# The sixth block of a per-head product, 40 rows and columns, or 120 that overlap the fifth

## The chip, the cores and the metric

The kernel runs on one core of one Trainium2 chip. The metric is the device time of one execution in microseconds, the median of several runs. Before the change it is 207.66 us (three runs, 207.59 to 207.98).

## What is computed

```python
xn = layernorm(x)                                   # x: 1 x 2048 x 640
q, k, v = split(xn @ wqkv)                          # 32 heads of 20 columns each
phi = lambda t: where(t > 0, t + 1, exp(t)) + 1e-6
pq, pk = phi(q), phi(k)
kv  = einsum("bhsd,bhse->bhde", pk, v)              # one 20 x 20 matrix per head
z   = einsum("bhsd->bhd", pk)
num = einsum("bhqd,bhde->bhqe", pq, kv)
den = einsum("bhqd,bhd->bhq", pq, z)[..., None] + 1e-6
attn  = (num / den) @ wo                            # heads joined to 640 columns
dense = gelu(xn @ w1 + b1) @ w2 + b2                # 640 -> 1536 -> 640
out = x + attn + dense                              # bfloat16 in and out
```

## The kernel before

The 2048 tokens are 16 tiles of 128, the 640 columns 5 tiles of 128. A small planner records every instruction of each engine in the order of the program text, works out which semaphores it has to wait for, and emits each engine's list as it stands. So the order on each engine is the order in which the Python code calls it. PSUM is eight banks of 512 fp32 columns, given out in turn by `take`; a matmul that gets a bank waits until its last reader is done.

TensorE goes through these stages one after the other:

- from 0 to 60 us: layernorm, transposes, and the first dense layer with gelu (`h_unit`, L357).
- 60 to 82: the keys, `phi(xn @ wk)` for 16 token tiles (L494), stored in PK.
- 82 to 104: GT, the product of the normalized tokens and PK over all tokens (L530), 640 x 640. The values are never formed: kv of a head is `wv.T @ GT` for that head's columns.
- 104 to 130: the queries in four chunks of 512 tokens (`q_chunk`, L542, 25 matmuls with 512 moving columns each). After a chunk's matmuls into one bank, `phi` runs on ScalarE (exp, L481) and VectorE (L482, L484) and leaves PQ.
- Between chunks 0 and 1, `kvt_step` makes the kv matrices. Inside chunk 2, after each of its five column tiles, `mt_block(nb)` multiplies them by 128 columns of wo.
- 130 to 205: the output. For each token tile, twelve pairs of matmuls with W2 and five with Msb (L643, the last tile in L679); in between, `den_step` (L590) gives the denominators, whose inverse is spread by a DMA (`rden_dma`) and multiplied into PQ (`rden_scale`). `x_again` reads x once more for the residual sum, after the last query matmul.

The 32 heads are cut into blocks of six heads, that is GW = 120 columns; 640 columns are NG = 6 blocks, five of 120 columns and a last one of gw[5] = 40 (two heads). `kvt_step` computes for block i, over five contraction tiles k, `Wqkv[v columns of i].T @ GT[columns of i]` into a 120 x 120 piece of a bank (40 x 40 for the last block). Blocks 0 to 3 go into one bank, blocks 4 and 5 into the next (`parts`). VectorE then multiplies with `maskKV`, a band of 20 x 20 ones along the diagonal, since only a head's own columns count, and writes KVT (L565): once for blocks 0 to 3, once for block 4, once for block 5.

`mt_block(nb)` has one matmul per block, with `Wo[rows of i, 128 columns]` as the stationary operand and KVT[i] as the moving one (L574): the contraction is over the block's 120 rows, 40 in the last. ScalarE copies the first bank to MT (L581), VectorE the second (L584), and a transposing DMA puts it into Msb (L586). The Wo rows come in two DMAs on SP's queue: blocks 0 to 4, then block 5; after them only W2 is queued among the weights.

In a matmul's shape, `128*40` in the profile is the stationary operand, 128 contraction rows and 40 columns, and `128x40` the moving operand, 40 columns long.

Of the kernel before, what the change touches and what calls it, by code (L numbers as in the profile page):

```python
# [5 lines left out]
ALU = AluOpType  # L6
ACT = mybir.ActivationFunctionType
P = 128
# [104 lines left out]
def bass_parallel_sum__linear_attn_block__dense_activation_gelu__prompt_kernel(  # L113
    nc: bass.Bass, A_x, A_wqkv, A_wo, B_x, B_w1, B_b1, B_w2, B_b2, out):
    Batch, S, D = A_x.shape
# [17 lines left out]
    GW = 6 * DH  # L133
    NG = -(-D // GW)
    gw = [min(GW, D - GW * i) for i in range(NG)]

    with contextlib.ExitStack() as es:
        sb = lambda *a, **k: es.enter_context(nc.sbuf_tensor(*a, **k))
# [13 lines left out]
        KVT = W1f[:, DT * D:DT * D + NG * GW].rearrange("p (g d) -> p g d", g=NG)  # L152
        MT = W1f[:, DT * D + NG * GW:DT * D + NG * GW + DT * D].rearrange("p (b d) -> p b d", b=DT)
        Wqkv = sb("Wqkv", [P, DT, 3 * D], BF16)
        W2 = sb("W2", [P, JT, D], BF16)
        Wo = sb("Wo", [P, NG, D], BF16)
# [9 lines left out]
        maskKV = sb("maskKV", [P, GW], BF16)  # L166
# [17 lines left out]
        def take(n):  # L184
            b = ring[0]
            if n == 2 and b % 2:
                b += 1
            b %= 8
            ring[0] = (b + n) % 8
            return b  # L190

        def bank(b, lo=0, hi=512):
            return ps[:, b * 512 + lo: b * 512 + hi]
# [16 lines left out]
        r_Wo = [R_("Wo%d" % i) for i in range(2)]  # L210
# [25 lines left out]
        def dma_w(eng, dst, src, res):  # L236
            Pl.ins(eng, lambda e: e.dma_start(dst, src), writes=[res], dma=True)
# [23 lines left out]
        dma_w("sync", Wqkv[:, :, 2 * D:3 * D], wqv[:, :, 2 * D:3 * D], r_Wv)  # L261
        dma_w("sync", b2bc[:], B_b2.rearrange("(a d) -> a d", a=1).partition_broadcast(P).rearrange("p a d -> p (a d)"), r_b2)
        dma_w("sync", Wo[0:GW, 0:NG - 1, :], A_wo[0:GW * (NG - 1), :].rearrange("(g p) n -> p g n", p=GW), r_Wo[0])
        dma_w("sync", Wo[0:gw[-1], NG - 1, :], A_wo[GW * (NG - 1):D, :], r_Wo[1])
        dma_w("sync", W2[:], B_w2.rearrange("(k p) n -> p k n", p=P), r_W2)

        g = "gpsimd"
# [221 lines left out]
        for t in range(NT):  # L489
            b = take(2)  # L490
# [36 lines left out]
        for f in range(DT):  # L527
            b = take(2)
# [24 lines left out]
        def kvt_step():  # L553
            for gs in parts:
                b = take(1)
                Pl.ins("tensor", [(lambda e, k=k, i=i, b=b, g0=gs[0]: e.matmul(  # L556
                    bank(b, GW * (i - g0), GW * (i - g0) + gw[i])[0:gw[i], :],
                    Wqkv[:, k, 2 * D + GW * i:2 * D + GW * i + gw[i]],
                    GTb[:, k, GW * i:GW * i + gw[i]], start=(k == 0), stop=(k == DT - 1)))
                    for i in gs for k in range(DT)], reads=[r_Wv] + r_GT, writes=[B_[b]])  # L560
                for lo, hi, w in ([(0, G1, GW)] if gs[0] == 0 else [(G1, NG - 1, GW), (NG - 1, NG, gw[-1])]):
                    n = hi - lo
                    src = bank(b, GW * (lo - gs[0]), GW * (lo - gs[0]) + n * w)[0:w, :].rearrange("p (g d) -> p g d", g=n)
                    msk = maskKV[0:w, 0:w].unsqueeze(1).to_broadcast([w, n, w])
                    Pl.ins(v, lambda e, lo=lo, hi=hi, w=w, src=src, msk=msk: e.tensor_tensor(  # L565
                        out=KVT[0:w, lo:hi, 0:w], in0=src, in1=msk, op=ALU.mult),
                        reads=[B_[b], r_masks], writes=[r_KVT] + r_W1)

        def mt_block(nb):
            for h, gs in enumerate(parts):  # L570
                b = take(1)
                n = gw[gs[0]] * (len(gs) - 1) + gw[gs[-1]]
                m0, m1 = GW * gs[0] // DT, (GW * gs[0] + n) // DT
                Pl.ins("tensor", [(lambda e, i=i, b=b, g0=gs[0]: e.matmul(  # L574
                    bank(b, GW * (i - g0), GW * (i - g0) + gw[i]), Wo[0:gw[i], i, nb * P:(nb + 1) * P],
                    KVT[0:gw[i], i, 0:gw[i]], start=True, stop=True)) for i in gs],
                    reads=r_Wo + [r_KVT], writes=[B_[b]])
                dst = MT[:, nb, :].rearrange("p (j m) -> p j m", j=DT)[:, :, m0:m1]
                src = bank(b, 0, n).rearrange("p (m j) -> p j m", j=DT)
                if h == 0:  # L580
                    Pl.ins("scalar", lambda e, dst=dst, src=src: e.activation(dst, src, ACT.Copy),  # L581
                           reads=[B_[b]], writes=[r_MT[nb][h]])
                else:
                    Pl.ins(v, lambda e, dst=dst, src=src: e.tensor_copy(dst, src),  # L584
                           reads=[B_[b]], writes=[r_MT[nb][h]])
            Pl.ins("sync", lambda e: e.dma_start_transpose(Msb[:, :, nb * P:(nb + 1) * P], MT[:, nb, :]),  # L586
                   reads=r_MT[nb], writes=[r_M[nb]] + ([r_zsum, r_zhl] if nb == 0 else []), dma=True)
# [37 lines left out]

        q_chunk(0)
        kvt_step()
        q_chunk(1)
        q_chunk(2, mt_block)
        q_chunk(3)  # L630
        for c in range(NC):
# [17 lines left out]
        def out_w2(t, lo=0, hi=JT, b=None):  # L649
            b = take(2) if b is None else b  # L650
            for i in range(lo, hi):
                Pl.ins("tensor", [mm(b, t, i, 0), mm(b, t, i, 1)], reads=mm_reads(t, i), writes=B_[b:b + 2],
                       mark=(i == JT - 1))
            return b
# [47 lines left out]
        for t in range(4, NT - 1):  # L702
            b = out_w2(t)
# [47 lines left out]
```

## Time and profile before

| | us |
|---|---|
| median of three runs | 207.66 |
| profiled execution | 208.03 |
| its span, first to last instruction | 206.8 |
| TensorE, weight loads busy | 139.4 |
| VectorE busy | 113.2 |
| ScalarE busy | 72.5 |
| L542, query matmuls, busy | 22.4 |
| L556, `kvt_step` matmuls, from 109.0 to | 110.8 |
| L574, first of `mt_block`, starts at | 117.2 |
| L574, last of `mt_block`, starts at | 123.9 |

The profile is of one execution, which took 208.03 us, 1.2 more than its span and 0.37 more than the median. Its lines give a start, a length and a count; a line of the timeline with a count over one runs from the first one's start to the last one's end. PE is the matmuls, PEld the weight loads that run beside them. Matmuls are pipelined and their recorded ends are modelled, so two records can overlap: where one instruction keeps the next one back, it is seen in the starts. The granted TensorE clock was 1.0.

### The profile page before, as it was taken

Reading aid. Unit: us, or ns where it says so; the run is one execution under the profiler, and the core shown is the slowest. Engines: PE = TensorE matmul, PEld = TensorE weight load, DVE = VectorE, ACT = ScalarE, POOL = GpSimd, SP = SyncE. Lnnn points to the kernel's source line nnn. Section 1 sums busy time; section 2 is a strip of 40 time slices with the busy share of each in tenths; the row PEclk is TensorE's granted clock in tenths of the full one; section 3 lists DMA queues with packets and bytes.
Section 4 is the critical chain, followed back from the end, with each engine's and each line's share of the span. In section 5 each row is a group of like instructions: output and inputs, shape, how many; then the busy total and the mean of one; then the engine's idle time right before and its main releaser. Section 6 shows DMA issues by size and latency. Waiting matters only on the chain.

```text
span 206.8 us, 3760 instructions
## 1 busy us (share of the span) xinstructions
PE 203.0 (98%) x1510; PEld 139.4 (67%) x1517; DVE 113.2 (55%) x231; ACT 72.5 (35%) x136; POOL 15.0 (7%) x46
## 2 busy tenths in 40 slices
PE   7999999999999999999999999999999999999996
PEld 2799987444457777777756565577777777777775
DVE  4668777200007888999288878474593522522332
ACT  3588887666676555111153566100000000000000
POOL 3143344300000000000000000000000000000000
PEclk9999999999999999999999999999999999999999
DMA  6993844599930000000300034682212111010002
GB/s 182 354 348 70 71 95 87 85 348 275 305 111 0 0 3 0 0 0 3 63 0 2 3 72 87 202 305 54 67 63 59 61 41 55 32 35 32 32 35 65
DMA packets 26579, 19.13 MB, mean 93 GB/s; under 512 B 13761, under 2 KB 26561, under 8 KB 26561
## 3 DMA queue, kind: packets, MB, share of 16 engines
q1 hardware_dynamic: 26265, 18.62, 32.7%
q10 hardware_dynamic: 296, 0.27, 0.5%
q8 instruction: 12, 0.20, 0.4%
q14 instruction: 6, 0.05, 0.1%
HBM read 12.62 MB, written 2.62 MB: 74 GB/s over the span
## 4 chain that ended last, share of the span: by engine, by line
PE 96%; DVE 1%; DMA 1%; issue 0%; DVEq 0%
PE ps L643 34%; PE ps L357 24%; PE ps L542 11%; PE ps L530 11%; PE ps L494 11%; PE ps L679 2%; PE ps L389 1%; DMA xPK<-in_A_x_dram 1%; PE ps L574 1%; DVE stats L313 1%; PE ps L556 1%; PE ps L590 1%; PE ps L378 0%; PE ps L341 0%; PE ps L300 0%
## 5 line engine op out<-in xcount | busy, mean ns | idle before, releaser
L643 PE MATMUL ps<-W,HG 128*128 128x320 bf16 x360 | 51.0, 299 | 0.0
L357 PE MATMUL ps<-xnT,W 128*128 128x256 bf16 (+2 forms) x382 | 50.4, 293 | 0.2
L643 PEld LDWEIGHTS ps<-W,HG 128*128 128x128 bf16 x360 | 35.1, 98 | 14.2 <-issue 0.4
L357 PEld LDWEIGHTS ps<-xnT,W 128*128 128x128 bf16 x385 | 33.8, 98 | 15.9
L361 ACT ACTIVATE HG<-ps,b1c 128x256 bf16<-128x256 f32 (+2 forms) x77 | 38.0, 515 | 12.7 <-PE ps L357 10.3
L662 DVE TENSOR_TENSOR out_sb<-ps,xnT 128x640 bf16<-128x640 f32 x15 | 12.4, 824 | 34.9 <-PE ps L643 34.6
L481 ACT ACTIVATE ek<-ps 128x512 bf16<-128x512 f32 (+1 forms) x36 | 23.2, 644 | 20.7 <-PE ps L542 11.5
L482 DVE TENSOR_SCALAR ek<-ek 128x512 bf16<-128x512 bf16 (+1 forms) x36 | 11.0, 307 | 27.4 <-ACT ek L481 26.1
L542 PE MATMUL ps<-xnT,Wqkv 128*128 128x512 bf16 x96 | 22.4, 381 | 0.3 <-issue 0.2
L643 PE MATMUL ps<-Msb,PQ 128*128 128x320 bf16 x150 | 22.3, 299 | 0.0
L494 PE MATMUL ps<-Wqkv,xnT 128*128 128x320 bf16 x160 | 21.9, 299 | 0.0
L530 PE MATMUL ps<-xPK,xn_tm 128*128 128x320 bf16 x160 | 21.9, 299 | 0.0
L494 PEld LDWEIGHTS ps<-Wqkv,xnT 128*128 128x128 bf16 x160 | 15.6, 98 | 6.3
L530 PEld LDWEIGHTS ps<-xPK,xn_tm 128*128 128x128 bf16 x160 | 15.6, 98 | 6.1
L643 PEld LDWEIGHTS ps<-Msb,PQ 128*128 128x128 bf16 x150 | 14.6, 98 | 5.7
L542 PEld LDWEIGHTS ps<-xnT,Wqkv 128*128 128x128 bf16 x100 | 11.3, 118 | 8.7
L313 DVE BATCH_NORM_STATS2 stats<-xPK 128x6 f32<-128x320 bf16 x32 | 14.7, 470 | 2.7 <-DMA xPK<-in_A_x_dram 2.7
L484 DVE SCALAR_TENSOR_TENSOR PQ<-ps,ek 128x512 bf16<-128x512 f32 x20 | 13.8, 692 | 2.1
L484 DVE SCALAR_TENSOR_TENSOR xPK<-ps,ek 128x640 bf16<-128x640 f32 x16 | 13.2, 824 | 1.7
L517 DVE TENSOR_TENSOR Msb<-Msb,xPK 128x640 f32<-128x640 f32 x14 | 11.6, 826 | 0.5
L323 POOL TENSOR_TENSOR rstd<-aggr,mhalf 128x1 f32<-128x1 f32 x16 | 9.1, 567 | 15.8 <-DVE aggr L321 15.8
L534 ACT ACTIVATE W<-ps 128x640 bf16<-128x640 f32 x5 | 3.5, 703 | 18.2 <-PE ps L530 18.2
(61 smaller groups left out, 92.7 us busy)
## 6 DMA issues: line engine op xcount, KB each, us to landing
xnT<-in_A_x_dram SPq DMA_DIRECT2D x4, 640.0 KB, 6.8
Wqkv<-in_A_wqkv_dram SPq DMA_DIRECT2D x3, 800.0 KB, 6.6
out_dram<-out_sb SPq DMA_DIRECT2D x15, 160.0 KB, 1.8
W<-in_B_w_dram SPq DMA_DIRECT2D x1, 1920.0 KB, 14.9
W<-in_B_w_dram SPq DMA_DIRECT2D x2, 640.0 KB, 7.4
xPK<-in_A_x_dram SPq DMA_DIRECT2D x2, 640.0 KB, 9.1
Wo<-in_A_wo_dram SPq DMA_DIRECT2D x1, 750.0 KB, 11.8
xPK<-in_A_x_dram SPq DMA_DIRECT2D x4, 160.0 KB, 4.6
```

The costliest lines, as they stand in the source:

```text
L313: Pl.ins(v, lambda e: e.bn_stats(stats[:, s, 6 * h:6 * h + 6], x_in[:, t, h * HW:(h + 1) * HW]), reads=[r_x[t]], writes=[r_stats[s][h]])
L357: Pl.ins("tensor", [(lambda e, k=k: e.matmul(bank(b, 0, w), W1[:, k, jb * P:(jb + 1) * P], xnT[:, k, tok], start=(k == 0), stop=(k == DT - ...
L361: Pl.ins("scalar", lambda e: e.activation(HG[:, jb, tok], bank(b, 0, w), ACT.Gelu_apprx_tanh, bias=b1c[:, jb:jb + 1]), reads=[B_[b], r_b1c ...
L481: Pl.ins("scalar", lambda e: e.activation(e2, src, ACT.Exp), reads=br, writes=[r_ek[s]])
L482: Pl.ins(v, lambda e: e.tensor_scalar(et, et, 1.0, 1e-6, ALU.min, ALU.add), reads=[r_ek[s]], writes=[r_ek[s]])
L484: Pl.ins(v, lambda e: e.scalar_tensor_tensor(out=d2, in0=src, scalar=0.0, in1=e2, op0=ALU.max, op1=ALU.add), reads=br + [r_ek[s]], writes= ...
L494: fns.append(lambda e, k=k, h=h, b=b, t=t: e.matmul(bank(b + h, 0, HW), xnT[:, k, t * P:(t + 1) * P], Wqkv[:, k, D + h * HW:D + (h + 1) * ...
L517: Pl.ins(v, lambda e, t=t: e.tensor_tensor(out=zsum, in0=zsum, in1=PK[:, t, :], op=ALU.add), reads=[r_PK[t], r_zsum], writes=[r_zsum])
L530: Pl.ins("tensor", [(lambda e, t=t, h=h, b=b, f=f: e.matmul(bank(b + h, 0, HW), xn_tm[:, t, f * P:(f + 1) * P], PK[:, t, h * HW:(h + 1) * ...
L542: Pl.ins("tensor", [(lambda e, k=k, j=j, b=b: e.matmul(bank(b), Wqkv[:, k, j:D:DT], xnT[:, k, cc], start=(k == 0), stop=(k == DT - 1))) fo ...
L643: return lambda e: e.matmul(bank(b + h, 0, HW), l, r[:, h * HW:(h + 1) * HW], start=(i == 0), stop=(i == JT + DT - 1))
L662: Pl.ins(v, lambda e: e.tensor_tensor(out=halves(out_sb[:, s, :]), in0=pair(b), in1=halves(x_res[:, t, :]), op=ALU.add), reads=B_[b:b + 2] ...
```

## The change

A list `ge` gives the first column of each block: GW * i for the first five, and D - GW = 520 in place of 600 for the sixth. The sixth block's stationary operand in `kvt_step` is now columns 520 to 639 of wv, 120 of them, so its product has 120 rows; its moving operand is still the 40 columns 600 to 639 of GT. The mask for it is columns 80 to 119 of `maskKV` with all 120 rows: its first 80 rows are zero and its last 40 are the diagonal blocks. KVT[5] then is 120 x 40. In `mt_block` the sixth matmul contracts over these 120 rows with rows 520 to 639 of wo, which is what the second Wo DMA now brings (150 KB in place of 50). Rows 520 to 599 meet zeros there.

```diff
     gw = [min(GW, D - GW * i) for i in range(NG)]
+    ge = [min(GW * i, D - GW) for i in range(NG)]
...
-        dma_w("sync", Wo[0:gw[-1], NG - 1, :], A_wo[GW * (NG - 1):D, :], r_Wo[1])
+        dma_w("sync", Wo[0:GW, NG - 1, :], A_wo[ge[-1]:D, :], r_Wo[1])
...
                 Pl.ins("tensor", [(lambda e, k=k, i=i, b=b, g0=gs[0]: e.matmul(
-                    bank(b, GW * (i - g0), GW * (i - g0) + gw[i])[0:gw[i], :],
-                    Wqkv[:, k, 2 * D + GW * i:2 * D + GW * i + gw[i]],
+                    bank(b, GW * (i - g0), GW * (i - g0) + gw[i])[0:GW, :],
+                    Wqkv[:, k, 2 * D + ge[i]:2 * D + ge[i] + GW],
                     GTb[:, k, GW * i:GW * i + gw[i]], start=(k == 0), stop=(k == DT - 1)))
                     for i in gs for k in range(DT)], reads=[r_Wv] + r_GT, writes=[B_[b]])
                 for lo, hi, w in ([(0, G1, GW)] if gs[0] == 0 else [(G1, NG - 1, GW), (NG - 1, NG, gw[-1])]):
                     n = hi - lo
-                    src = bank(b, GW * (lo - gs[0]), GW * (lo - gs[0]) + n * w)[0:w, :].rearrange("p (g d) -> p g d", g=n)
-                    msk = maskKV[0:w, 0:w].unsqueeze(1).to_broadcast([w, n, w])
+                    src = bank(b, GW * (lo - gs[0]), GW * (lo - gs[0]) + n * w)[0:GW, :].rearrange("p (g d) -> p g d", g=n)
+                    msk = maskKV[0:GW, GW * lo - ge[lo]:GW * lo - ge[lo] + w].unsqueeze(1).to_broadcast([GW, n, w])
                     Pl.ins(v, lambda e, lo=lo, hi=hi, w=w, src=src, msk=msk: e.tensor_tensor(
-                        out=KVT[0:w, lo:hi, 0:w], in0=src, in1=msk, op=ALU.mult),
+                        out=KVT[0:GW, lo:hi, 0:w], in0=src, in1=msk, op=ALU.mult),
                         reads=[B_[b], r_masks], writes=[r_KVT] + r_W1)
...
                 Pl.ins("tensor", [(lambda e, i=i, b=b, g0=gs[0]: e.matmul(
-                    bank(b, GW * (i - g0), GW * (i - g0) + gw[i]), Wo[0:gw[i], i, nb * P:(nb + 1) * P],
-                    KVT[0:gw[i], i, 0:gw[i]], start=True, stop=True)) for i in gs],
+                    bank(b, GW * (i - g0), GW * (i - g0) + gw[i]), Wo[0:GW, i, nb * P:(nb + 1) * P],
+                    KVT[0:GW, i, 0:gw[i]], start=True, stop=True)) for i in gs],
                     reads=r_Wo + [r_KVT], writes=[B_[b]])
```

In the changed kernel every line after the new one has a number higher by one: L542 becomes L543, L556 becomes L557, L574 becomes L575.

## The prediction

> **What bounds the kernel now.** I read the page's busy table and chain of waits first, then TensorE's groups, then the timeline of the stretch from 108 to 125 us where the change lies, and last the same timeline in slits a few hundredths of a microsecond wide, which print one or two instructions each.
>
> ```profile
> PE 203.0 (98%) x1510; PEld 139.4 (67%) x1517; DVE 113.2 (55%) x231; ACT 72.5 (35%) x136; POOL 15.0 (7%) x46
> PE 96%; DVE 1%; DMA 1%; issue 0%; DVEq 0%
> L643 PE MATMUL ps<-Msb,PQ 128*128 128x320 bf16 x150 | 22.3, 299 | 0.0
> ```
>
> TensorE is 96% of the chain that ends last, and L643, which follows the changed stretch, shows no idle time. So a tenth taken from TensorE's stream at 110 us is a tenth at the end, and work on other engines counts only if it makes TensorE wait. But "busy" hides pauses here: a matmul's record (299 ns in L643) is longer than the distance to the next one, and the records overlap. I therefore measure from start to start. First what lies around one `mt_block` (columns: start, length, engine, line, names, shape, count):
>
> ```profile
> 117.00 0.38 PE L542 MATMUL ps<-xnT,Wqkv 128*128 128x512 bf16 x1
> 117.21 0.32 PE L574 MATMUL ps<-W,Wo 120*128 120x120 bf16 x3
> 117.42 0.34 PE L574 MATMUL ps<-W,Wo 120*128 120x120 bf16 x2
> 117.57 0.19 PE L574 MATMUL ps<-W,Wo 40*128 40x40 bf16 x1
> 117.69 0.41 PE L542 MATMUL ps<-xnT,Wqkv 128*128 128x512 bf16 x1
> 117.94 0.38 PE L542 MATMUL ps<-xnT,Wqkv 128*128 128x512 bf16 x1
> 118.16 0.38 PE L542 MATMUL ps<-xnT,Wqkv 128*128 128x512 bf16 x1
> ...
> 117.57 0.09 PEld L574 LDWEIGHTS ps<-W,Wo 40*128 40x128 bf16 x1
> 117.69 0.12 PEld L542 LDWEIGHTS ps<-xnT,Wqkv 128*128 128x128 bf16 x1
> ```
>
> The 512-column matmuls of L542 follow each other at 0.216 (117.94 to 118.16). The three 120-column ones span 0.32, less one record of 0.215 (the group's mean), over two distances: 0.052 each. The step from 128 rows to 120 costs nothing: 117.00 to 117.21 is L542's usual distance. The step from 120 rows to 40 does: the next weight load, and with it the 40-row matmul, starts only at 117.57, 0.15 after the fifth 120-row matmul instead of 0.052. The step back does too: 0.12 to L542's first, and that one needs 0.25 instead of 0.216 to its second. The blocks begin at 117.21, 118.81, 120.40, 121.99 and 123.59 in the timeline, so all five repeat this to 0.01.
>
> `kvt_step`, once, is the same with the columns of the array:
>
> ```profile
> 110.33 0.34 PE L556 MATMUL ps<-W,Wqkv 128*120 128x120 bf16 x2
> 110.48 0.30 PE L556 MATMUL ps<-W,Wqkv 128*40 128x40 bf16 x5
> 110.55 0.23 PE L556 MATMUL ps<-W,Wqkv 128*40 128x40 bf16 x3
> 110.95 0.38 PE L542 MATMUL ps<-xnT,Wqkv 128*128 128x512 bf16 x1 [0.18 <-issue]
> 110.28 0.14 PEld L556 LDWEIGHTS ps<-W,Wqkv 128*120 128x120 bf16 x1
> 110.48 0.10 PEld L556 LDWEIGHTS ps<-W,Wqkv 128*40 128x40 bf16 x1
> 110.70 0.12 PEld L542 LDWEIGHTS ps<-xnT,Wqkv 128*128 128x128 bf16 x1
> 109.28 0.38 PE L556 MATMUL ps<-W,Wqkv 128*120 128x120 bf16 x4
> ```
>
> The last line gives the 120-wide distance: (0.38 - 0.218) / 3, 0.054 to 0.055; the third one that of the last 40-wide ones: (0.23 - 0.18) / 2 = 0.025. From the last 120-wide load to the first 40-wide one it is 0.20. L542's first load starts at 110.70; its matmul has no record (96 of 100 are in the trace), and the one printed at 110.95 is its second.
>
> **What the Trainium skill says.** "TensorEngine Tiling (Array Packing)", Key Properties: changing the tiling mode, not just the tile, drains TensorE; its list of configurations has 64-row and 64-column ones, into which 40 rows or columns fit and 120 don't. That reads like the pauses above, on both sides of each 40; the trace agrees in place, and the page gives no price. "TensorE: Matmul & The Clock Gate", LDWEIGHTS: a load's time goes with its columns, not with its contraction rows. The trace agrees: 92 ns for 40x128 beside a median of 96 in that line, but 95 for 128x40 against 135 for 128x120. The same page, Weight-path perf modes: fast loading needs the full 128 columns; the trace agrees, 98 ns for 128*128 against 135 for 128*120.
>
> **The change part by part.** Its profiled execution took 208.03 us, its span 206.8; the 1.2 around the span I keep. The median of the runs is 207.66, so I make the sum as a difference and take it off both.
>
> Instructions: none is added, removed or moved. Each engine's list has the same instructions in the same order with the same waits; only shapes differ.
>
> (1) `mt_block`, five times: the 40-row matmul becomes a 120-row one, with the same 128-column load and the same 40 moving columns. From the fifth matmul to L542's second it now takes 117.94 - 117.42 = 0.52. Without a change of mode: 0.052 for the fifth, then e for the sixth, then 0.216. The short matmul's own distance e isn't shown at 120 rows. From below it is 0.025, the distance of the 40-column ones in `kvt_step`; from above 0.055, the 120-wide neighbours. I take 0.04, since L542's strided load behind it takes 117 ns where an unstrided one takes 98. So 0.52 - 0.308 = 0.21 each, 5 x 0.21 = 1.05 us; the ends are 5 x 0.197 = 0.98 and 5 x 0.227 = 1.13.
>
> (2) `kvt_step`, once: five 128x120 loads under 40 moving columns. Now, from the last 120-wide matmul (110.33) to L542's second (110.95), 0.62. After: 0.055 for the last old one, 5 distances, 0.216. The load has the length of its neighbours (135 ns), and those run at 0.055, so I take 0.055 for four and 0.04 for the last: 0.055 + 0.22 + 0.04 + 0.216 = 0.53, a gain of 0.09. From below, with 0.025 each: a gain of 0.22. From above, if a load with only 40 columns to hide it is seen whole, 0.135 each: 0.055 + 0.675 + 0.216 = 0.95, a loss of 0.32.
>
> (3) VectorE, L565: 40x40 becomes 120x40 with a mask slice 80 columns in. 40 columns per partition as before, so 0.19 us; at most the 0.28 of the 120x120 one. The timeline has L565 done at 112.6, its reader starts at 117.0: 4.4 us of cover.
>
> (4) DMA: the second Wo transfer grows from 50 to 150 KB. At the 348 GB/s that the page's fullest slice shows, 100 KB is 0.3 us; its issue on SP's queue (0.50 now) may grow to the 0.92 of b2's 128 rows. Behind it only W2 is queued, issued at 44.44 and landing 14.9 later, at 59.3; first read at 129.5 by L643. Wo is first read at 117.0. Nothing at the end; without this cover it would cost under 1 us.
>
> (5) What is late next: with 1.38 us per block in place of 1.59, VectorE's part of `q_chunk(2)` comes near. Its starts go 119.64 (L482), 120.03 (L484), 120.64 (L584, 0.31): 1.31 per block, under 1.38, and a matmul needs a bank freed two or three blocks earlier. Behind, `den_step` starts at 132.85, 1.4 after VectorE's last PQ at 131.4. The Msb transposes have landed by about 130 and are read at 143.8. x_again, rden and its DMA are started by TensorE's own progress and move with it.
>
> Sum: 1.05 + 0.09 = 1.14 us. Profiled execution 208.03 - 1.14 = 206.89, span 205.7; median 207.66 - 1.14 = 206.52, said as 206.5.
>
> **Rivals.**
> - One edge stays. The pause after the 40 may belong to the short stream, which can't hide L542's 117 ns load; only the entry goes: 5 x (0.15 - 0.052) = 0.5, `kvt_step` even: 207.2 at most, 207.1 with some of (2). For it: L542's load starts late, at 117.69. Against: the short ones of L556 hide 95 ns loads at 0.025 each. 8%.
> - VectorE or ScalarE paces `q_chunk(2)`. If a block takes VectorE 1.45, at most 5 x 0.07 = 0.35 comes back: 206.9. For: 1.31 of 1.38. Against: the free banks. 7%.
> - The change doesn't do what it says: the pauses come from something kept, a wait for a bank or the 40 moving columns, and 207.6 to 207.7 results. For: a wait stands before L542's load. Against: a 0.15 and 0.12 equal in five blocks is no semaphore's habit, and the waits list nothing for TensorE there but 0.2 of issue. 6%.
> - Slower: the pauses stay as in the last case, and a 120-wide load doesn't overlap a 40-column matmul at all. Then each of L556's five pairs takes load plus matmul, 0.135 + 0.18 = 0.315: 0.055 + 5 x 0.315 + 0.216 = 1.85 instead of 0.62, 1.2 lost, 208.9. It decides from a distance of 0.155, where the loss reaches 0.42. For: 40 columns are little cover. Against: 25 like loads run at 0.055. 4%.
>
> **How the numbers follow.** The forecast has 75%, the rivals 8, 7, 6 and 4. About 0.2% (0.42 us) is what a measurement of this kernel can tell from no change; faster then means under 207.24. The forecast and nearly all of the first two cases lie there: 0.88; the third gives same, 0.08 with the weaker ends of the first two; slower 0.04. The bounds of (1) and (2) give 206.3 to 207.0 (1.13 + 0.22 gained, or 0.98 - 0.32); with the runs' own spread (207.59 to 207.98) and the partial cases I take 206.1 to 207.2.
>
> **What would show it.** In the changed profile, L575's sixth matmul should start about 0.05 after the fifth, L543's first 0.03 to 0.06 later, and the blocks should come every 1.38 us. L557's five short ones should run at 0.055 and L543's "issue" 0.18 vanish. A block of 1.48 would be the one-edge case, 1.59 no effect; a distance over 0.1 in L557 the exposed load. I would be wrong in the mechanism if the pauses go and the span doesn't shrink by as much: then look for TensorE idle at L543 or `den_step`.

## The result, and the profile after

| | before | after |
|---|---|---|
| median, us | 207.65 (6 runs) | 206.60 (6 runs, 206.48 to 206.99) |
| ratio of the times | | 0.9948, 95% interval 0.9935 to 0.9961 |
| profiled execution, us | 208.03 | 206.48 |
| its span, us | 206.8 | 205.2 |

The change made the kernel faster by 1.05 us; the interval of the ratio allows 0.8 to 1.35. The page of the changed kernel still has TensorE as the bound:

```profile
PE 201.8 (98%) x1517; PEld 138.6 (68%) x1517; DVE 113.2 (55%) x231; ACT 72.5 (35%) x136; POOL 15.0 (7%) x46
L543 PE MATMUL ps<-xnT,Wqkv 128*128 128x512 bf16 x100 | 22.8, 380 | 0.0
```

The two spans differ by 1.6 us, more than the medians. Where that lies is read from the chain of waits in order of time (start, length, what). Before:

```profile
82.05 21.73 PE ps L530 x160
...
117.38 0.39 PE ps L574 x6
117.76 1.21 PE ps L542 x5
118.97 0.39 PE ps L574 x6
...
129.66 3.26 PE ps L643 x24
...
134.11 66.12 PE ps L643 x486
```

and after:

```profile
81.68 21.73 PE ps L531 x160
103.42 5.40 PE ps L543 x25
108.81 1.61 PE ps L557 x30
110.43 6.48 PE ps L543 x30
116.91 0.28 PE ps L575 x6
117.19 1.10 PE ps L543 x5
118.29 0.28 PE ps L575 x6
...
128.13 3.26 PE ps L644 x24
...
132.59 66.12 PE ps L644 x486
```

The GT matmuls start 0.37 earlier after than before. That comes from the first ten microseconds, where nothing was changed: the first dense layer's first matmul (L357, now L358) starts at 9.6 before and at 9.1 after. In the other runs below GT starts between 81.57 and 82.10, without regard to what was changed. From the end of GT (start plus 21.73) to the first output matmul it is 129.66 - 103.78 = 25.88 before and 128.13 - 103.41 = 24.72 after: 1.16 us. I call this the stretch; it leaves the start out, so it is the better measure for what follows. The output pieces behind it (66.12) are equal, so all of it reaches the end. In the chain of waits a block's two pieces went from 0.39 + 1.21 to 0.28 + 1.10.

Narrow slits of the timeline around the first block of the changed kernel:

```profile
116.53 0.38 PE L543 MATMUL ps<-xnT,Wqkv 128*128 128x512 bf16 x1
116.75 0.43 PE L575 MATMUL ps<-W,Wo 120*128 120x120 bf16 x5
116.96 0.24 PE L575 MATMUL ps<-W,Wo 120*128 120x120 bf16 x2
117.01 0.18 PE L575 MATMUL ps<-W,Wo 120*128 120x40 bf16 x1
117.04 0.39 PE L543 MATMUL ps<-xnT,Wqkv 128*128 128x512 bf16 x1
117.26 0.38 PE L543 MATMUL ps<-xnT,Wqkv 128*128 128x512 bf16 x1
```

The fifth matmul starts at 116.96, the sixth (120x40) 0.05 later, L543's first 0.03 after that, its second 0.225 later. The 0.15 and the 0.12 have gone. From the fifth to L543's second it is 0.31 where it was 0.52. And in the kv step:

```profile
109.97 0.40 PE L557 MATMUL ps<-W,Wqkv 128*120 128x120 bf16 x5
110.02 0.35 PE L557 MATMUL ps<-W,Wqkv 128*120 128x40 bf16 x4
110.05 0.32 PE L557 MATMUL ps<-W,Wqkv 128*120 128x40 bf16 x3
110.27 0.38 PE L543 MATMUL ps<-xnT,Wqkv 128*128 128x512 bf16 x1
110.49 0.38 PE L543 MATMUL ps<-xnT,Wqkv 128*128 128x512 bf16 x1
```

The last 120-wide matmul starts at 109.97 (its line holds the first four short ones too). The five short ones start at 110.02, 110.05 and then evenly up to L543's first at 110.27, four steps of 0.055. So the first of them follows the last 120-wide one at 0.055, where it was 0.15, and from that 120-wide one to L543's second it is 0.52 where it was 0.62. The "issue" of 0.18 behind the last short one is gone too, but it was no pause of its own: it stood where L542's first matmul had no record. The run mt_alone below keeps the kv step of before, has that record, and shows no "issue".

### The profile page after: what moved, and what is told of

The parts are those of the page before. It is cut to its first block, busy times and chain, and to the rows that moved or that the text cites. A ratio compares the mean times of both kernels' runs of the same rounds, so it can differ in the third digit from the quotient of the medians.

```text
span 205.2 us, 3767 instructions
## 1 busy us (share of the span) xinstructions
PE 201.8 (98%) x1517; PEld 138.6 (68%) x1517; DVE 113.2 (55%) x231; ACT 72.5 (35%) x136; POOL 15.0 (7%) x46
## 4 chain that ended last, share of the span: by engine, by line
PE 96%; DVE 1%; DMA 1%; issue 0%; DVEq 0%
PE ps L644 34%; PE ps L358 24%; PE ps L495 11%; PE ps L531 11%; PE ps L543 11%; PE ps L680 2%; PE ps L390 1%; DMA xPK<-in_A_x_dram 1%; DVE stats L314 1%; PE ps L557 1%; PE ps L575 1%; PE ps L591 1%; PE ps L379 0%; PE ps L342 0%; DVE xn_tm L372 0%
## 5 line engine op out<-in xcount | busy, mean ns | idle before, releaser
L358 PE MATMUL ps<-xnT,W 128*128 128x256 bf16 (+2 forms) x385 | 50.6, 294 | 0.0
L358 PEld LDWEIGHTS ps<-xnT,W 128*128 128x128 bf16 x385 | 33.8, 98 | 16.0 <-DMA W<-in_B_w_dram 0.2
L482 ACT ACTIVATE ek<-ps 128x512 bf16<-128x512 f32 (+1 forms) x36 | 23.2, 644 | 19.6 <-PE ps L543 10.4
L483 DVE TENSOR_SCALAR ek<-ek 128x512 bf16<-128x512 bf16 (+1 forms) x36 | 11.0, 307 | 26.3 <-ACT ek L482 24.8
L543 PE MATMUL ps<-xnT,Wqkv 128*128 128x512 bf16 x100 | 22.8, 380 | 0.0
L543 PEld LDWEIGHTS ps<-xnT,Wqkv 128*128 128x128 bf16 x100 | 11.3, 118 | 8.5
L324 POOL TENSOR_TENSOR rstd<-aggr,mhalf 128x1 f32<-128x1 f32 x16 | 9.1, 567 | 15.8 <-DVE aggr L322 15.8
## 6 DMA issues: line engine op xcount, KB each, us to landing
W<-in_B_w_dram SPq DMA_DIRECT2D x1, 1920.0 KB, 15.8
```

The source lines that it names most:

```text
L358: Pl.ins("tensor", [(lambda e, k=k: e.matmul(bank(b, 0, w), W1[:, k, jb * P:(jb + 1) * P], xnT[:, k, tok], start=(k == 0), stop=(k == DT - ...
L482: Pl.ins("scalar", lambda e: e.activation(e2, src, ACT.Exp), reads=br, writes=[r_ek[s]])
L483: Pl.ins(v, lambda e: e.tensor_scalar(et, et, 1.0, 1e-6, ALU.min, ALU.add), reads=[r_ek[s]], writes=[r_ek[s]])
L543: Pl.ins("tensor", [(lambda e, k=k, j=j, b=b: e.matmul(bank(b), Wqkv[:, k, j:D:DT], xnT[:, k, cc], start=(k == 0), stop=(k == DT - 1))) fo ...
```

## The experiments

Theory, "mode": a stationary tile of at most 64 rows, or of at most 64 columns, puts the array into another mode than a larger one, and TensorE drains at each change between the two. The number of changes counts, not the short matmul. Rivals: the pause grows with the rows and columns that are missing ("size"); the short matmul is slow itself, wherever it stands; only one of the two steps matters. All times in this table are from the runs with that label; the runs of the kernel before beside them had a median of 207.88 (the first four) and 207.82 (the last four), so the ratios are to be compared, not the medians. A block's period is the distance of the L574 rows (L575, L576, L578) in the timeline.

| label | median, us | ratio to before (95%) | stretch, us | block's period, us |
|---|---|---|---|---|
| (before) | | 1 | 25.88 | 1.59 |
| (after) | 206.60 | 0.9948 (0.9935 to 0.9961) | 24.72 | 1.38 |
| rows60 | 208.02 | 0.9995 (0.9972 to 1.0018) | 25.91 | 1.59 |
| rows80 | 206.70 | 0.9942 (0.9925 to 0.9960) | 24.66 | 1.38 |
| mt_alone | 206.82 | 0.9943 (0.9927 to 0.9959) | 24.82 | 1.38 |
| kvt_alone | 207.73 | 0.9991 (0.9976 to 1.0006) | 25.78 | 1.59 |
| apart40 | 209.05 | 1.0060 (1.0038 to 1.0082) | 27.03 | 1.82 |
| beside40 | 207.94 | 1.0006 (0.9995 to 1.0017) | 26.01 | 1.62 |
| apart120 | 206.87 | 0.9953 (0.9938 to 0.9969) | 24.85 | 1.41 |
| wide128 | 206.48 | 0.9931 (0.9913 to 0.9950) | 24.55 | 1.38 |

In apart120 the chain leaves TensorE in this stretch, so the end of GT is taken from the timeline there: its last matmul starts at 103.30 and is 0.30 long.

### One size changed: 60 and 80

```diff
-    ge = [min(GW * i, D - GW) for i in range(NG)]
+    gr = [GW] * (NG - 1) + [60]
+    ge = [min(GW * i, D - gr[i]) for i in range(NG)]
...
-                    bank(b, GW * (i - g0), GW * (i - g0) + gw[i])[0:GW, :],
-                    Wqkv[:, k, 2 * D + ge[i]:2 * D + ge[i] + GW],
+                    bank(b, GW * (i - g0), GW * (i - g0) + gw[i])[0:gr[i], :],
+                    Wqkv[:, k, 2 * D + ge[i]:2 * D + ge[i] + gr[i]],
...
-                    bank(b, GW * (i - g0), GW * (i - g0) + gw[i]), Wo[0:GW, i, nb * P:(nb + 1) * P],
-                    KVT[0:GW, i, 0:gw[i]], start=True, stop=True)) for i in gs],
+                    bank(b, GW * (i - g0), GW * (i - g0) + gw[i]), Wo[0:gr[i], i, nb * P:(nb + 1) * P],
+                    KVT[0:gr[i], i, 0:gw[i]], start=True, stop=True)) for i in gs],
```

This is rows60, on the changed kernel; rows80 has 80 in place of 60. The mask, the VectorE product and the Wo transfer follow with gr in the same way.

> The changed kernel with the sixth block 60 columns and rows tall instead of 120 (both steps; it overlaps the fifth by one head). Theory (mode: a stationary tile of at most 64 rows or columns puts the array into another mode, and each change drains it): 60 fits 64, so all pauses come back: sixth matmul of a block 0.15 after the fifth, first query matmul 0.12 later, blocks every 1.59, and 207.6 us as before the change. Rival (size: the pause grows with the rows and columns that are missing from 120): a quarter of it goes, blocks every 1.54, 207.4 us. Rival (any deviation from 120 costs the whole pause): 207.6 as well, told apart by rows80.

> The same with 80 rows and columns. Theory (mode): 80 doesn't fit 64, so no pause: blocks every 1.38, and the five short matmuls of the kv step follow their 80-column loads at about 0.037 to 0.04 instead of 0.055, 0.09 saved: 206.5 us. Rival (size): half of the pause is left, blocks every 1.49, 207.1 us. Rival (any deviation): blocks every 1.59, 207.6 us.

Slits of the timeline of rows60, first block (the first line holds the fifth and the sixth), then the kv step:

```profile
116.98 0.34 PE L576 MATMUL ps<-W,Wo 120*128 120x120 bf16 x2
117.25 0.41 PE L544 MATMUL ps<-xnT,Wqkv 128*128 128x512 bf16 x1
...
110.00 0.33 PE L558 MATMUL ps<-W,Wqkv 128*60 128x40 bf16 x5
110.26 0.41 PE L544 MATMUL ps<-xnT,Wqkv 128*128 128x512 bf16 x1
```

and of rows80, the same places:

```profile
116.85 0.18 PE L576 MATMUL ps<-W,Wo 80*128 80x40 bf16 x1
116.88 0.39 PE L544 MATMUL ps<-xnT,Wqkv 128*128 128x512 bf16 x1
...
109.96 0.31 PE L558 MATMUL ps<-W,Wqkv 128*80 128x40 bf16 x4
110.11 0.38 PE L544 MATMUL ps<-xnT,Wqkv 128*128 128x512 bf16 x1
```

In rows60 the sixth matmul's record, some 0.19 long as that of 40 rows was, ends at 117.32, so it starts at 117.13, 0.15 after the fifth at 116.98; L544 follows 0.12 later with the longer record, 0.41. That is the picture of 40 rows to the hundredth, though 20 rows more are there. In rows80 it is 0.03 from the short one to L544, and no pause is left. So the pause is whole at 60 and absent at 80: "size" falls, and so does "any deviation from 120". A bound at 64 fits; sizes between 60 and 80 weren't tried.

The two runs also price the column side. Their stretches differ by 25.91 - 24.66 = 1.25; the blocks give 5 x 0.21 = 1.05; the remaining 0.20 is one trip into the narrow mode and back in the kv step. As the short matmuls there follow each other at 0.03 with 60 columns and at 0.038 with 80, the trip alone is by estimate some 0.03 more.

### One step alone

```diff
         def kvt_step():
+            Pl.ins(v, lambda e: e.memset(KVT[0:GW, NG - 1, 0:gw[-1]], 0.0), writes=[r_KVT] + r_W1)
...
-                    bank(b, GW * (i - g0), GW * (i - g0) + gw[i]), Wo[0:gw[i], i, nb * P:(nb + 1) * P],
-                    KVT[0:gw[i], i, 0:gw[i]], start=True, stop=True)) for i in gs],
+                    bank(b, GW * (i - g0), GW * (i - g0) + gw[i]), Wo[0:GW, i, nb * P:(nb + 1) * P],
+                    KVT[0:GW, i, 0:gw[i]], start=True, stop=True)) for i in gs],
```

This is mt_alone, made from the kernel before; a further small DMA fills the Wo rows that meet the zeros. kvt_alone is made from the changed kernel:

```diff
-                    bank(b, GW * (i - g0), GW * (i - g0) + gw[i]), Wo[0:GW, i, nb * P:(nb + 1) * P],
-                    KVT[0:GW, i, 0:gw[i]], start=True, stop=True)) for i in gs],
+                    bank(b, GW * (i - g0), GW * (i - g0) + gw[i]), Wo[(64 if i == NG - 1 else 0):GW, i, nb * P:(nb + 1) * P],
+                    KVT[(64 if i == NG - 1 else 0):GW, i, 0:gw[i]], start=True, stop=True)) for i in gs],
```

> The kernel before with the second step alone changed: the sixth matmul of each block contracts over 120 rows, of which KVT rows 40 to 119 are set to zero by one VectorE memset; the kv step keeps its 40-wide loads. Theory: 5 x 0.21 goes, the kv step keeps its 0.62: 206.7 us. Rival (the kv step's row mode is what drags the blocks along, or the gain is one edge): 207.1 to 207.6 us.

> The changed kernel, but the sixth matmul of each block contracts over rows 64 to 119 alone (the rows before are zero or not needed), 56 rows in the lower half of the array; the kv step has its 120-wide loads. Theory: a row tile of 64 again, so the blocks take 1.59 each and only the kv step's 0.10 is gained: 207.55 us. Rival (the pause comes from starting at row 0 with few rows, or from the short kv loads): blocks every 1.38, 206.6 us.

mt_alone saves 25.88 - 24.82 = 1.06 of the stretch, kvt_alone 0.10; together 1.16, which is what the whole change saves. So no influence of one step on the other is seen. The 0.10 is seen in the trace alone: the times of kvt_alone can't be told from those of the kernel before. The slits of kvt_alone, first block, show the pauses with 56 rows that start at row 64:

```profile
117.52 0.19 PE L575 MATMUL ps<-W,Wo 56*128 56x40 bf16 x1
117.64 0.41 PE L543 MATMUL ps<-xnT,Wqkv 128*128 128x512 bf16 x1
```

From the short one to L543 it is 0.12 as before the change, with the record of 0.41. So it made no difference here where the rows begin, only that they are few.

### The same instructions in another order

```diff
-                    KVT[0:gw[i], i, 0:gw[i]], start=True, stop=True)) for i in gs],
+                    KVT[0:gw[i], i, 0:gw[i]], start=True, stop=True)) for i in (gs if h == 0 else (5, 4, 5))],
```

This is apart40, on the kernel before. beside40 has (4, 5, 5) in its place, and apart120 is the edit of apart40 made to the changed kernel.

> The kernel before, with the sixth block's 40-row matmul issued twice in each of the five blocks, once ahead of the fifth block's 120-row matmul and once behind it (the second writes the same numbers again). Theory (each change of mode is paid): two trips per block instead of one, 5 x (0.148 + 0.122 - 0.052) = 1.1 us more than before, up to 1.25 if the 0.03 behind the way back is paid too: 208.8 us, blocks every 1.81 to 1.84. Rival (a 40-row matmul itself is slow, wherever it stands): the same here, told apart by beside40.

> The same instructions as apart40, but the two 40-row matmuls stand side by side behind the fifth block's. Theory: one trip per block as before and one more short matmul in the same mode at about 0.025: 5 x 0.025 = 0.1 more than before, 207.8 us, blocks every 1.62. Rival (a 40-row matmul itself is slow): 0.15 to 0.21 more per block, 208.4 to 208.7 us.

> The changed kernel with the same doubling as apart40: the sixth block's matmul, now of 120 rows, before and behind the fifth's. Theory: no change of mode, so each costs a short matmul, 0.028 to 0.055 per block: 0.15 to 0.3 more than the changed kernel, 206.8 us, blocks every 1.41 to 1.44. Rival (the doubled issue itself or the short moving operand costs what apart40 shows): 207.7 us.

Slits of apart40, first block (the first line is the first of the two 40-row matmuls, the second line the other):

```profile
117.51 0.19 PE L574 MATMUL ps<-W,Wo 40*128 40x40 bf16 x1
117.79 0.19 PE L574 MATMUL ps<-W,Wo 40*128 40x40 bf16 x1
117.92 0.41 PE L542 MATMUL ps<-xnT,Wqkv 128*128 128x512 bf16 x1
```

and of beside40 (the first line holds both, the second the second alone):

```profile
117.42 0.21 PE L574 MATMUL ps<-W,Wo 40*128 40x40 bf16 x2
117.46 0.18 PE L574 MATMUL ps<-W,Wo 40*128 40x40 bf16 x1
117.57 0.41 PE L542 MATMUL ps<-xnT,Wqkv 128*128 128x512 bf16 x1
```

Both kernels issue the same seven matmuls per block. Apart, the second short one starts 0.28 after the first, with one 120-row matmul between them; side by side, 0.04 after it. The blocks come every 1.82 against 1.62, and before it was 1.59. The second short matmul costs 0.03 where it stands in the mode that is already set, and 0.23 where it needs a trip of its own: 5 x 0.20 = 1.0 us between two orders of the same work, 1.1 in the medians. With 120 rows the doubling costs 0.03 per block even when apart (1.41 against 1.38). "The short matmul is slow itself" falls.

### A version with 128 columns throughout

```diff
+    gr = [GW] * (NG - 1) + [P]
-    ge = [min(GW * i, D - GW) for i in range(NG)]
+    ge = [min(GW * i, D - P) for i in range(NG)]
...
+        band(mask5[:], r_masks, -(GW * (NG - 1) - ge[-1]), (1, DH), [(DH, 2), (0, DH)])
...
-                    bank(b, GW * (i - g0), GW * (i - g0) + gw[i])[0:GW, :],
-                    Wqkv[:, k, 2 * D + ge[i]:2 * D + ge[i] + GW],
+                    bank(b, GW * (i - g0), GW * (i - g0) + gw[i])[0:P, :],
+                    Wqkv[:, k, 2 * D + ge[i]:2 * D + ge[i] + P],
```

The edit is on the changed kernel. The last block's operand now begins at column 512, so its heads lie in rows 88 to 127 and need the mask mask5, made once on GpSimd; its Wo transfer, its product and its matmul in `mt_block` have 128 rows.

> The changed kernel with all stationary operands of the kv step 128 columns wide instead of 120 (the last from column 512 on, contracted over 128 rows in the blocks, with a mask of its own). Theory: a full 128-column load is the faster kind (97 ns against 135 in the trace), so the 25 long matmuls run at their own 0.052 instead of 0.055 and the five short ones at 0.028 instead of 0.055: 0.08 + 0.13 = 0.2 less than the changed kernel, 206.4 us, and no pause anywhere. Rival (the 0.055 isn't the load's): no difference, 206.6 us.

The chain of waits of wide128 has the kv step in 1.43, where the changed kernel has 1.61:

```profile
108.98 1.43 PE ps L560 x30
110.42 0.07 issue
```

The groups of weight loads, kept apart by shape, of wide128 and then of the changed kernel:

```profile
L560 PEld LDWEIGHTS ps<-W,Wqkv 128*128 128x128 bf16 x30 | 1.6, 98 | 0.2
```

```profile
L557 PEld LDWEIGHTS ps<-W,Wqkv 128*120 128x120 bf16 x30 | 1.8, 135 | 0.2
```

A load of 128 columns takes 98 ns, one of 120 takes 135. The last of the short matmuls in wide128:

```profile
110.19 0.23 PE L560 MATMUL ps<-W,Wqkv 128*128 128x40 bf16 x3
```

They follow each other at (0.23 - 0.18) / 2 = 0.025, where the changed kernel has 0.055. (L546's first matmul has no record in wide128, hence the "issue" of 0.07.) The stretch shrinks by 0.17, near the 0.2 expected. In the times it can't be told from the changed kernel: 0.9931 against 0.9948, with intervals that overlap. Against the kernel before it is faster by 0.7%.

## Why the prediction was right

The forecast was 206.5 us (206.1 to 207.2); 206.60 was measured. By its own steps:

1. `mt_block`, 0.21 each and 1.05 in all. Measured alone: 1.06. The term e, taken as 0.04 between 0.025 and 0.055, is 0.03 (117.01 to 117.04), and L543's second matmul comes 0.01 later than assumed; the two misses cancel, and the sum stands. The blocks come every 1.38, as said.
2. `kvt_step`, 0.09. Measured: 0.10. The one short distance among the five (0.03) came first and not last, which leaves the sum as it was. The sign of the vanished "issue" says nothing, since it came from the missing record. Two effects were netted here: a trip that costs 0.20, taken away, and loads of 120 columns that pace the short matmuls at 0.055 where the 40-wide ones ran at 0.025, which gives about half of it back. The bad end, a load seen whole at 0.135, did not come: four of the steps are 0.055, as with the 120-column neighbours. That a load's time goes with its columns held in direction alone: 95 ns at 40 columns, 135 at 120, and 98 at a full 128.
3. VectorE's L565 (now L566): it is done at 112.2 and its reader starts at 116.75. No cost.
4. DMA: the Wo transfer of 150 KB was covered, as argued; W2 landed 15.8 us after its issue in place of 14.9, far ahead of 128. (The highest slice of the page of before shows 354 GB/s, not 348; nothing hangs on it.)
5. What is late next: VectorE came close, as feared, and no closer. Its timeline in a middle block of the changed kernel, after a line of ScalarE's exp:

```profile
118.33 0.60 ACT L482 ACTIVATE ek<-ps 128x512 bf16<-128x512 f32 x1 [0.32 <-PE ps L543]
118.58 0.31 DVE L585 CAST W<-ps 128x160 bf16<-128x160 f32 x1
118.96 0.29 DVE L483 TENSOR_SCALAR ek<-ek 128x512 bf16<-128x512 bf16 x1
119.36 0.69 DVE L485 SCALAR_TENSOR_TENSOR PQ<-ps,ek 128x512 bf16<-128x512 f32 x1
119.96 0.32 DVE L585 CAST W<-ps 128x160 bf16<-128x160 f32 x1
```

From one L585 to the next it is 1.38, TensorE's own period, and TensorE shows no idle time in L543. VectorE still waits for ScalarE in each block, but more briefly: ScalarE's exp (118.33 + 0.60) ends 0.03 ahead of L483's start, as it did ahead of L482 before, and between L585's end (118.89) and L483's start (118.96) VectorE now stands idle for 0.07, where it was 0.27. That leaves the 1.31 which the prediction gave VectorE. What a block shorter by more than 0.07 would do, no run shows.

Of the rivals, "one edge stays" was wrong in the first block already: both edges went. "Doesn't do what it says" and "slower" needed pauses that stay; the 40 moving columns did stay, and the pauses went. "VectorE or ScalarE paces" needed TensorE to stand idle in L543. The sum by the trace (1.16) is 0.1 above the difference of the medians (1.05). The runs' spread is larger than this 0.1, and it isn't explained further.

What rests on argument: that it is the tiling mode in the sense of the Trainium skill ("TensorEngine Tiling (Array Packing)", Key Properties) that drains. The runs show the step between 60 and 80, that 40, 56 and 60 rows pay alike, from row 0 or row 64 on, and that changes are paid and not matmuls. No record names a mode.

## What to carry to other kernels

Look at the starts of short matmuls between large ones, not at the busy share: TensorE was 98% busy with 1.2 us of pauses inside. A stationary tile of 40 to 60 rows or columns amid full ones cost 0.2 us per trip here; pad it past that with rows that meet zeros (80 did), or put all such tiles side by side so that one trip serves them. Where the moving operand is short, columns padded to 120 gave about half of the gain back through longer loads; columns padded to the full 128 did not.

## What the runs showed of the hardware that was not expected

- A trip costs about the same in rows (0.21) as in columns (0.20, some 0.23 by the estimate above).
- Reordering seven matmuls of one block, with nothing added, moved the block by 0.20 us.
- Where little is moved, the load sets the pace of the short matmuls, and a full one is as quick as the narrowest: 0.025 behind 128x40 loads (before) and behind 128x128 ones (wide128), 0.038 behind 128x80 (rows80: from the second short one at 109.96 to L544 at 110.11 there are four steps), 0.055 behind 128x120.
- Each of the two changes of a trip, in and out, costs about 0.1 us by itself, and it doesn't take a short moving operand. `den_step`, which no run changed, has stationary operands of 32 columns under 512 moving ones, in groups of four that start almost together. In the kernel before:

```profile
132.21 0.71 PE L643 MATMUL ps<-W,HG 128*128 128x320 bf16 x4
132.62 0.30 PE L643 MATMUL ps<-W,HG 128*128 128x320 bf16 x1
132.85 1.26 PE L590 MATMUL ps<-PQ,ZB 128*32 128x512 bf16 x20
133.72 0.39 PE L590 MATMUL ps<-PQ,ZB 128*32 128x512 bf16 x4
134.04 0.31 PE L643 MATMUL ps<-W,HG 128*128 128x320 bf16 x1
```

From L643's last start to L590's first it is 0.23, where L643's own distance is (0.71 - 0.30) / 3 = 0.14. From the start of L590's last group to L643 it is 0.32, where the groups come every (1.26 - 0.39) / 4 = 0.22. That is 0.09 in and 0.10 out. In `mt_block` it was 0.15 - 0.052 = 0.10 in, and 0.12 less a short matmul's own 0.025, also 0.10, out. These two pauses of `den_step` are read, not tested: no run gives it wider tiles.
